# A chunked decay-attention and expert kernel: bonus and state products in quarters of the array, scaling by 1/q0 on ScalarE, another order on TensorE

## The chip, the cores and the metric

One core of a Trainium2 chip runs the kernel. Its engines are called as in the profile: PE is TensorE (PEld its weight loads), DVE is VectorE, ACT is ScalarE, POOL is GpSimd, and SP is the engine that issues most DMAs. The metric is the device time of one execution in microseconds, lower is better. The kernel before has a median of 321.75 us over three runs (320.64 to 328.07).

## What is computed

The first half is a linear attention with a decay that depends on time and channel, for 4 batches, 8 heads, 768 steps and 48 channels. The second sends each of the 3072 rows through at most one of eight small networks.

```python
for t in range(S):
    cur = einsum('bhd,bhe->bhde', u * k[t], v[t])
    y[t] = einsum('bhd,bhde->bhe', r[t], state + cur)
    state = w[t][..., None] * state + einsum('bhd,bhe->bhde', k[t], v[t])
...
logits = x @ w_gate;  e = argmax(logits);  p = softmax(logits)
out = x + (x @ w_skip > 0) * p[e] * (relu(x @ w1[e]) @ w2[e])
```

Everything is kept in fp32 or in pairs of numbers that add up to it.

## The kernel before

**Chunks.** The 768 steps of a batch are cut into 6 chunks of 128, so the attention is 24 chunks, one after the other. Within a chunk the channels of two heads lie on the 128 partitions, one head on 0 to 47 and the other on 64 to 111 (index g), and a counts four such pairs of heads. The state is carried from chunk to chunk; the first chunk of each batch starts without one.

**What one chunk takes.** The helpers have the names that the prediction uses.

- `prep_scan`, `prep_keys`: DVE runs two scans of products of w, `q` from the end (L277) and `rh` from the start (L289), and takes `rq`, 1/q at the chunk's start (L284). POOL makes `kq` = k q (L287).
[...]
- `intra`: PE transposes `kq` (L321), ACT copies the result to `kt` (L323), and PE forms the scores `kq` x `rp` in quarters of the array, 64 rows by 64 columns, into the banks psA0 and psA1 (L328).
- `mask`: DVE multiplies each of the two banks by a triangle, giving `asb` (L334).
- `bonus_sums`, `bonus`: PE multiplies `rk` by u and sums over the channels of each head, with a block-diagonal weight `ubk_sb`, into a bank psB (L343); DVE multiplies by v, held with channels on partitions (`vt`), into the bank psY (L347), which starts y.
- `update`, `carry`: PE adds k v to the state in psu (L356); ACT scales it by the next chunk's q (L366) and copies it to `sblk` (L371), block-diagonal again.
- `outputs`: PE adds `asb` x v (L378) and `sblk` x `rp` (L383) to psY. `evict`: ACT copies psY to `xT` (L388). `rows_out`: PE turns it into rows and router logits (L396). `store`: ACT copies those (L405, L408) and SP writes them out (L410).

**The order.** It is written by hand, in the loop at L595: every engine takes its instructions in the order of the program's text. In step s the loop loads chunk s+4, prepares chunk s+2 (scans and products), forms scores, masks and bonus of chunk s+1, and finishes the outputs of chunk s. On PE a step is update, outputs, transposes, scores, bonus sums, rows_out. On DVE it is the scan q, rq, rh, rp, two masks, bonus. An SP queue holds all chunk loads in program order; a DMA also waits for the one eight places before it, since there are eight semaphores for them.

**Beside the chunks.** After every six chunks a router (L412) finds each row's expert and its place. It is a generator of small steps: `drip` sets some of them between DVE's other work, `pace` says how many, and what they need of PE or ACT is queued in `held` and issued at `flush`. In the first two groups ACT makes the one-hot rows (`mark`, L479), two instructions each, two rows per chunk; later groups make them on DVE (`one_hot`, L474). In some chunks the weights of the first experts are fetched (L90), and ACT and POOL split them into a rounded part and a rest (L107, L273). After the last chunk the experts follow; their products of PE are most of the second half of the span.

## Time and profile before

| what | value |
|---|---|
| median of three runs | 321.75 us |
| the profiled execution | 317.5 us |
| its span, first to last instruction | 315.6 us |
| mean granted clock of PE | 0.986 |
| busy: PE, DVE, ACT, POOL | 292.2, 244.8, 185.3, 115.5 us |
| chain that ended last: PE, DMA, DVE | 72%, 13%, 10% |
| mean DMA rate over the span | 192 GB/s |

In the rows of a timeline stand the start in us from the span's start, the length, the engine, the line, the operation, output<-inputs, sizes as partitions x elements, and a count; in brackets the idle time ahead and what ended it. A row that stands for several instructions gives the time from the first one's start to the last one's end. Grouped rows give the total busy time and the mean length in ns of one, and after the bar the idle time ahead. A product of PE in fp32 shows as two instructions, so four products read x8, and a weight load goes with each. Records of one engine overlap a little, so the distance from start to start is what an instruction costs its engine.

### The profile page before, as it was taken

What the parts mean: (1) busy time and instruction counts of PE and PEld (TensorE: products, weight loads), DVE (VectorE), ACT (ScalarE), POOL (GpSimd) and SP (SyncE); (2) the same over time, 40 slices, a digit from 0 to 9 for tenths busy, and PEclk for the clock granted to TensorE, in tenths of its full rate; (3) what the DMA queues carried; (4) which work ended last, traced back from release to release, by engine and by line L of the source; (5) the groups of instructions that cost most, each with busy time, mean ns of one, the idle gap of its engine ahead of it and who ended that gap; (6) DMA issues with size and microseconds to landing.
All of it is one profiled execution on the core that took longest, in us unless ns stands there. A gap on an engine that the chain in (4) does not pass through costs nothing.

```text
span 315.6 us, 8456 instructions
## 1 busy us (share of the span) xinstructions
PE 292.2 (93%) x3229; PEld 269.6 (85%) x3229; DVE 244.8 (78%) x505; ACT 185.3 (59%) x527; POOL 115.5 (37%) x118
## 2 busy tenths in 40 slices
PE   7499999899898998979999999999999999999992
PEld 2388888788787887868889899999999999999991
DVE  8899999999999999999637479587785949496310
ACT  4437667689775998766633358274564828184200
POOL 8164455555535566543401772411102020101111
PEclk9879999999999999999999999999999999999998
DMA  7999999999899988885301489756657473630001
GB/s 227 220 214 241 232 292 271 257 264 264 212 233 257 267 187 179 180 206 194 116 25 34 143 294 348 275 195 218 213 199 239 152 256 95 243 143 27 6 4 37
DMA packets 23778, 60.45 MB, mean 192 GB/s; under 512 B 4902, under 2 KB 11338, under 8 KB 23728
## 3 DMA queue, kind: packets, MB, share of 16 engines
q1 hardware_dynamic: 21248, 53.69, 62.6%
q0 software_dynamic: 2048, 5.48, 5.3%
q8 instruction: 27, 0.44, 0.7%
q10 hardware_dynamic: 432, 0.66, 0.6%
q14 instruction: 23, 0.19, 0.2%
HBM read 52.76 MB, written 7.86 MB: 192 GB/s over the span
## 4 chain that ended last, share of the span: by engine, by line
PE 72%; DMA 13%; DVE 10%; POOL 1%; issue 1%; ACT 1%; SPq 0%; POOLq 0%; DVEq 0%
DMA wrk<-wrk 10%; PE psO L790 7%; PE psO L788 7%; PE psO L789 7%; PE psY L378 6%; PE psH L770 6%; PE psH L769 6%; PE psH L768 6%; PE psA L328 6%; PE psY L383 5%; PE psB L343 5%; DVE asb L334 4%; PE psH L126 4%; DVE psY L347 3%; PE psT L321 3%; DVE rp L297 2%
## 5 line engine op out<-in xcount | busy, mean ns | idle before, releaser
L775 ACT ACTIVATE hh<-psH 128x256 fp32r<-128x256 f32 x60 | 23.0, 383 | 56.8 <-PE psH L770 53.5
L732 POOL DMA_INDIRECT out<-fin,ids x16 | 17.0, 1065 | 102.5 <-DVE fin L795 94.7
L770 PE MATMUL psH<-xTh,w1l 128*128 128x256 f32 x168 | 47.6, 283 | 0.0
L769 PE MATMUL psH<-xTl,w1h 128*128 128x256 f32 x168 | 47.6, 283 | 0.0
L768 PE MATMUL psH<-xTh,w1h 128*128 128x256 f32 x168 | 47.6, 283 | 0.0
L302 POOL TENSOR_TENSOR rk<-wrk 128x512 f32<-128x512 f32 x24 | 30.6, 1275 | 28.9 <-DVE rp L297 14.5
L788 PE MATMUL psO<-w2h,hh 128*128 128x384 f32 x120 | 40.8, 340 | 0.0
L790 PE MATMUL psO<-w2h,hl 128*128 128x384 f32 x120 | 40.2, 335 | 0.0
L789 PE MATMUL psO<-w2l,hh 128*128 128x384 f32 x120 | 40.2, 335 | 0.0
L378 PE MATMUL psY<-asb,v 128*48 128x128 f32 x384 | 26.6, 282 | 13.1 <-DVE psY L347 13.0
L287 POOL TENSOR_TENSOR kq<-wrk,q 128x512 f32<-128x512 f32 x24 | 28.6, 1190 | 18.5 <-DVE q L277 13.4
L776 DVE SCALAR_TENSOR_TENSOR hl<-psH,hh 128x256 fp32r<-128x256 f32 x60 | 25.2, 420 | 12.5 <-ACT hh L775 12.1
L334 DVE TENSOR_TENSOR asb<-psA,c_sb 128x512 f32<-128x512 f32 x48 | 30.7, 681 | 4.3 <-PE psA L328 4.3
L378 PEld LDWEIGHTS psY<-asb,v 128*48 128x48 f32 x384 | 20.5, 126 | 15.6 <-DVE psY L347 15.4
L297 DVE SCALAR_TENSOR_TENSOR rp<-wrk,rq,rh 128x128 f32<-128x128 f32 x96 | 33.1, 405 | 0.5
L770 PEld LDWEIGHTS psH<-xTh,w1l 128*128 128x128 f32 x168 | 32.2, 192 | 0.0
L769 PEld LDWEIGHTS psH<-xTl,w1h 128*128 128x128 f32 x168 | 32.2, 192 | 0.0
L768 PEld LDWEIGHTS psH<-xTh,w1h 128*128 128x128 f32 x168 | 32.2, 192 | 0.0
L795 DVE SCALAR_TENSOR_TENSOR fin<-psO,gates,xg 128x384 f32<-128x384 f32 x15 | 9.3, 618 | 28.5 <-PE psO L790 28.5
L289 DVE TENSOR_TENSOR_SCAN rh<-wrk,pss 128x516 f32<-128x516 f32 x24 | 28.9, 1205 | 2.6 <-PE pss L516 1.3
L277 DVE TENSOR_TENSOR_SCAN q<-wrk,pss 128x516 f32<-128x516 f32 x24 | 29.1, 1214 | 1.4 <-DMA wrk<-wrk 1.4
L343 PE MATMUL psB<-rk,ubk_sb 128*128 128x128 f32 x192 | 27.8, 288 | 0.9 <-POOL rk L302 0.9
(145 smaller groups left out, 668.6 us busy)
## 6 DMA issues: line engine op xcount, KB each, us to landing
r<-w SPq DMA_DIRECT2D x48, 512.0 KB, 5.8
wrk<-wrk SPq DMA_DIRECT2D x46, 288.9 KB, 6.3
v<-vN SPq DMA_DIRECT2D x24, 192.0 KB, 6.2
out<-x SPq DMA_DIRECT2D x24, 192.0 KB, 5.4
vt<-wrk SPq DMA_DIRECT2D x46, 96.0 KB, 6.1
wrk<-wrk SPq DMA_DIRECT2D x1, 258.5 KB, 3.8
wrk<-wrk ACTq DMA_DIRECT2D x1, 256.0 KB, 4.0
wrk<-wrk SPq DMA_DIRECT2D x1, 256.0 KB, 4.5
```

What stands on the lines that cost most here:

```text
L277: nc.vector.tensor_tensor_scan(q.rearrange("p a j -> p (a j)")[:, ::-1], t[:, 1:1 + NP * CW][:, ::-1], floor, 0.0, op0=ALU.mult, op1=ALU.max)
L297: last = nc.vector.scalar_tensor_tensor(rp[:, a], wk["r"][:, a], wk["rq"][:, a], wk["rh"][:, a, :P], op0=ALU.mult, op1=ALU.mult)
L302: mul = nc.gpsimd.tensor_tensor(rk.rearrange("p a j -> p (a j)"), wk["w"][:, R_OFF:K_OFF], wk["w"][:, K_OFF:V_OFF], op=ALU.mult)
L334: nc.vector.tensor_tensor(s, psa[g], tri.rearrange("p (o j) -> p o j", o=1).to_broadcast([P, NP, P]), op=ALU.mult)
L343: nc.tensor.matmul(wk["psb"][:, a], ubk_sb[:, a], wk["rk"][:, a], start=True, stop=True)
L378: nc.tensor.matmul(psy[64 * g:64 * g + D, a], v[:, 2 * a + g], wk["asb"][g][:, a], start=False, stop=(c == 0), skip_group_check=True)
L768: nc.tensor.matmul(ps, w1h[:, o:o + P], xTh[:, kc], start=(kc == 0), stop=False)
L769: nc.tensor.matmul(ps, w1h[:, o:o + P], xTl[:, kc], start=False, stop=False)
L770: nc.tensor.matmul(ps, w1l[:, o:o + P], xTh[:, kc], start=False, stop=(kc == KC - 1))
L788: nc.tensor.matmul(pso, h[j, fc][0], w2h[:, o], start=(fc == 0), stop=False)
L789: nc.tensor.matmul(pso, h[j, fc][0], w2l[:, o], start=False, stop=False)
L790: nc.tensor.matmul(pso, h[j, fc][1], w2h[:, o], start=False, stop=(fc == FC - 1))
```

## The change

**Quarters.** `ubk_sb` holds u in 64 columns instead of a block-diagonal 128, and the bonus sums become eight products of 64 rows by 64 columns for one chunk instead of four over the whole array (L353). They go into the right halves of psA0 and psA1, from which DVE's masks of the same chunk have been read by then. psB is gone. The state's part of y becomes eight such products too (L400), with `sblk` no longer block-diagonal and copied by one instruction. y lies in two banks, psY0 and psY1, one for each g; the pairs of heads 0, 1 lie on partitions 0 to 47 and 2, 3 on 64 to 111. So bonus (L359) and evict (L407) are two instructions each of 128x256, `vt` is loaded in this layout by four DMAs of 1 KB rows instead of two of 2 KB rows, and the matrix `wgp_sb` by twelve DMAs instead of three.

**1/q0 onto r.** ACT writes r rq into `rp`, four instructions of 128x128 (L296, `scale_reads`), and DVE multiplies by rh in one instruction of 128x512 (L301).

**Order.** Bonus sums and bonus move from the step of the scores to the next step; rows_out moves from the end of a step to the start of the next. The router's one-hot rows are all made on DVE, and its pace for the third group is 3 instead of 2. The small product that POOL makes of the split weights is set beside the bonus of an earlier chunk.

In the rows that follow, tiles carry numbers that tell buffers apart; a scan reads as SCALAR_TENSOR_TENSOR. On DVE, from one chunk's bonus to the next, before:

```order
L347 TENSOR_TENSOR psY<-psB_250,vt_86 128x512
L277 SCALAR_TENSOR_TENSOR q_279<-wrk_85,pss 128x516
L284 RECIPROCAL rq_289<-q_279 128x4
L289 SCALAR_TENSOR_TENSOR rh_293<-wrk_85,pss 128x516
L297 SCALAR_TENSOR_TENSOR rp_295<-wrk_85,rq_289,rh_293 128x128 x4
L334 TENSOR_TENSOR asb_1_327<-psA_110,c_sb 128x512
L334 TENSOR_TENSOR asb_1_329<-psA_111,c_sb 128x512
L347 TENSOR_TENSOR psY<-psB_331,vt_87 128x512
```

and now:

```order
L359 TENSOR_TENSOR psY_109<-psA_111,vt_86 128x256
L359 TENSOR_TENSOR psY_110<-psA_112,vt_86 128x256
L276 SCALAR_TENSOR_TENSOR q_300<-wrk_85,pss 128x516
L283 RECIPROCAL rq_317<-q_300 128x4
L288 SCALAR_TENSOR_TENSOR rh_321<-wrk_85,pss 128x516
L301 TENSOR_TENSOR rp_326<-rp_326,rh_321 128x512
L339 TENSOR_TENSOR asb_1_350<-psA_111,c_sb 128x512
L339 TENSOR_TENSOR asb_1_352<-psA_112,c_sb 128x512
L359 TENSOR_TENSOR psY_109<-psA_111,vt_87 128x256
L359 TENSOR_TENSOR psY_110<-psA_112,vt_87 128x256
```

The bonus that follows the masks belonged to the masks' own chunk in the same step; it still follows them, but in the next step, in two halves, and it reads the banks psA (111 and 112) that the masks have read. The four rp instructions are one.

On ACT, from one chunk's store to its checks, before:

```order
L405 COPY lgs_351<-psX_531 128x18
L408 COPY x_543<-psX_531 128x2x96 x2
L366 ACTIVATE psu<-psu,q_466 128x48 x4
L371 COPY sblk_112<-psu 64x4x48 x2
L388 COPY xT_588<-psY 128x512
L323 COPY kt_595<-psT_590 128x512
L311 ACTIVATE junk_623,viol<-wrk_85,bias_lo 128x512
L313 COPY q0all<-q_561 128x4
```

and now:

```order
L424 COPY lgs_370<-psX_578 128x18
L427 COPY x_584<-psX_578 128x2x2x48 x2
L380 ACTIVATE psu<-psu,q_505 128x48 x4
L383 COPY sblk_113<-psu 128x4x48
L325 COPY kt_618<-psT_613 128x512
L407 COPY xT_642<-psY_109 128x256
L407 COPY xT_642<-psY_110 128x256
L296 ACTIVATE rp_645<-wrk_85,rq_636 128x128 x4
L313 ACTIVATE junk_673,viol<-wrk_85,bias_lo 128x512
L315 COPY q0all<-q_611 128x4
```

The transposed kq (kt) is copied ahead of xT instead of behind it, xT is two rows, and four scalings rp stand between xT and the checks (junk, q0all).

On PE, one chunk from its bonus sums or rows_out to the next scores, before:

```order
L343 MATMUL psB_427<-rk_300,ubk_sb 128x128 x4
L396 MATMUL psX_436<-wgp_sb,xT_398 128x105 x4
L356 MATMUL psu<-v_205,kt_405 48x48 x8
L378 MATMUL psY<-asb_2_423,v_205 48x128
L378 MATMUL psY<-asb_2_425,v_205 48x128 x2
...
L383 MATMUL psY<-rp_295,sblk_112 128x128 x4
L321 MATMUL psT_495<-c_sb,kq_387 128x128 x4
L328 MATMUL psA_110<-rp_391,kq_387 64x128
L328 MATMUL psA_111<-rp_391,kq_387 64x128
```

and now, with L353 and L400 standing for eight rows each:

```order
L415 MATMUL psX_472<-wgp_sb,xT_430 128x105 x4
L370 MATMUL psu<-v_220,kt_406 48x48 x8
L353 MATMUL psA_111<-rk_332,ubk_sb 64x2x64
L353 MATMUL psA_112<-rk_332,ubk_sb 64x2x64
...
L323 MATMUL psT_507<-c_sb,kq_426 128x128 x4
L392 MATMUL psY_109<-asb_2_457,v_220 48x128 x4
L392 MATMUL psY_110<-asb_2_459,v_220 48x128 x4
L400 MATMUL psY_109<-rp_326,sblk_113 48x128
L400 MATMUL psY_110<-rp_326,sblk_113 48x128
...
L333 MATMUL psA_111<-rp_433,kq_426 64x128
L333 MATMUL psA_112<-rp_433,kq_426 64x128
```

The bonus sums stood behind the scores and ahead of rows_out; they now stand behind rows_out and update, and the transposes between them and the outputs.

The core of the difference; the parts left out set up tiles, rename the recording helper `vec` to `nc.vector`, and rename banks.

```diff
@@ loads
                 return
             for g in range(2):
                 nc.sync.dma_start(t[64 * g:64 * g + D], wrk[b, c, g, :, :V_OFF])
-            for g in range(2):
-                nc.sync.dma_start(vf[64 * g:64 * g + D], wrk[b, c, g, :, V_OFF:V_OFF + NP * P])
+
+        def load_vt(i):
+            b, c = seq[i]
+            vt = vt_sb[i % (NBUF + 1)]
+            for c2 in range(2):
+                for g in range(2):
+                    o = V_OFF + 2 * c2 * P
+                    nc.sync.dma_start(vt[64 * c2:64 * c2 + D, 2 * g:2 * g + 2],
+                                      wrk[b, c, g, :, o:o + 2 * P])
...
@@ tiles
-        ubk_sb = keep.tile([P, NP, P], F32, name="ubk_sb")
+        ubk_sb = keep.tile([P, NP, HP], F32, name="ubk_sb")
...
-        psy = ps1.tile([P, NP, P], F32, tag="psY", name="psY")
+
+
+        psy = [ps1.tile([P, 512], F32, tag=f"psY{g}", name=f"psY{g}") for g in range(2)]
+        psy3 = [z[:, :2 * P].rearrange("p (b j) -> p b j", b=2) for z in psy]
         psa = [ps1.tile([P, NP, P], F32, tag=f"psA{g}", name=f"psA{g}") for g in range(2)]
-        sblk = [pers.tile([P, NP, 2, HP], F32, name=f"sblk{i}") for i in range(2)]
+        sblk = [pers.tile([P, NP, HP], F32, name=f"sblk{i}") for i in range(2)]
...
@@ prep
-                if vec.last is not None:
-                    beside(mul, vec.last)
+                beside(nc.gpsimd.tensor_tensor(lo, raw, hi, op=ALU.subtract), work[i - 2]["bonus"])
...
-        def prep_reads(i):
+        def scale_reads(i):
             wk = work[i]
             rp = wk["rp"] = att.tile([P, NP, P], F32, tag="rp", name=f"rp{i}", bufs=3)
             for a in range(NP):
-                last = nc.vector.scalar_tensor_tensor(
-                    rp[:, a], wk["r"][:, a], wk["rq"][:, a], wk["rh"][:, a, :P],
-                    op0=ALU.mult, op1=ALU.mult)
+                nc.scalar.activation(rp[:, a], wk["r"][:, a], AF.Copy, scale=wk["rq"][:, a])
+
+        def prep_reads(i):
+            wk = work[i]
+            rp = wk["rp"]
+            last = nc.vector.tensor_tensor(rp, rp, wk["rh"][:, :, :P], op=ALU.mult)
...
@@ products
+        psb = [z.rearrange("p a (h j) -> p a h j", h=2)[:, :, 1] for z in psa]
+
         def bonus_sums(i):
-            wk = work[i]
-            wk["psb"] = ps1.tile([P, NP, P], F32, tag="psB", name=f"psB{i}")
-            for a in range(NP):
-                nc.tensor.matmul(wk["psb"][:, a], ubk_sb[:, a], wk["rk"][:, a],
-                                 start=True, stop=True)
+            rk = work[i]["rk"].rearrange("p a (h j) -> p a h j", h=2)
+            for a2 in range(2):
+                for c2 in range(2):
+                    for g in range(2):
+                        a, rows = 2 * c2 + a2, slice(64 * g, 64 * g + HP)
+                        nc.tensor.matmul(psb[g][64 * c2:64 * c2 + HP, 2 * a2:2 * a2 + 2],
+                                         ubk_sb[rows, a], rk[rows, a], start=True, stop=True)
 
         def bonus(i):
-            nc.vector.tensor_tensor(psy, work[i]["psb"], vt_sb[i % (NBUF + 1)], op=ALU.mult)
+            vt = vt_sb[i % (NBUF + 1)].rearrange("p a (h j) -> p (a h) j", h=2)
+            for g in range(2):
+                work[i]["bonus"] = nc.vector.tensor_tensor(
+                    psy[g][:, :2 * P].rearrange("p (q j) -> p q j", j=HP), psb[g],
+                    vt[:, 4 * g:4 * g + 4], op=ALU.mult)
...
             nb = sblk[(i + 1) % 2]
-            for g in range(2):
-                rows = slice(64 * g, 64 * g + HP)
-                nc.scalar.copy(nb[rows, :, g, :D], psu[rows, :, :D])
+            nc.scalar.copy(nb[:, :, :D], psu[:, :, :D])
 
         def outputs(i):
             b, c = seq[i]
             wk, v = work[i], v_sb.pop(i)
-            for a in range(NP):
-                for g in ((0, 1), (1, 0))[a % 2]:
-                    nc.tensor.matmul(psy[64 * g:64 * g + D, a], v[:, 2 * a + g],
-                                     wk["asb"][g][:, a], start=False, stop=(c == 0),
-                                     skip_group_check=True)
+            for g in range(2):
+                for a2 in range(2):
+                    for c2 in range(2):
+                        a = 2 * c2 + a2
+                        nc.tensor.matmul(psy3[g][64 * c2:64 * c2 + D, a2], v[:, 2 * a + g],
+                                         wk["asb"][g][:, a], start=False, stop=(c == 0),
+                                         skip_group_check=True)
             if c > 0:
-                for a in range(NP):
-                    nc.tensor.matmul(psy[:, a], sblk[i % 2][:, a], wk["rp"][:, a],
-                                     start=False, stop=True, skip_group_check=True)
+                for a2 in range(2):
+                    for c2 in range(2):
+                        for g in range(2):
+                            a, rows = 2 * c2 + a2, slice(64 * g, 64 * g + HP)
+                            nc.tensor.matmul(psy3[g][64 * c2:64 * c2 + D, a2],
+                                             sblk[i % 2][rows, a, :D], wk["rp"][rows, a],
+                                             start=False, stop=True, skip_group_check=True)
 
         def evict(i):
-            xT = work[i]["xT"] = att.tile([P, NP, P], F32, tag="xT", name=f"xT{i}")
-            nc.scalar.copy(xT, psy)
+            xT = work[i]["xT"] = att.tile([P, 2 * 2, P], F32, tag="xT", name=f"xT{i}")
+            for g in range(2):
+                nc.scalar.copy(xT[:, 2 * g:2 * g + 2], psy3[g])
...
@@ router
-            def mark(c):
-                dd = att.tile([P, 2 * P], BF16, tag="dd", name=f"dd{i0}_{c}")
-                hot = att.tile([P, 2 * P], BF16, tag="hot", name=f"hot{i0}_{c}", bufs=NC)
-                nc.scalar.activation(dd, iota, AF.Square, bias=r1[:, c], scale=-1.0)
-                nc.scalar.activation(hot, dd, AF.Relu, bias=rows1_, scale=-2.0)
-                hots.append(hot)
...
-                if i0 + m >= LATE:
-                    one_hot(c)
-                    yield 1
-                else:
-                    marks.append(lambda c=c: mark(c))
+                one_hot(c)
+                yield 1
...
@@ the loop
                 if s == -1:
                     nc.sync.dma_start(wgs_sb, wgs)
                 if on(s - 1):
+                    rows_out(s - 1)
                     store(s - 1)
+                if on(s):
+                    update(s)
+                    carry(s)
+                    bonus_sums(s)
+                drip(pace[0])
                 for i0, m in GROUPS:
                     if i0 + m == s:
-                        pace[0] = 1 if i0 + m < LATE else 2
+                        pace[0] = 1 if i0 + m < LATE else 3
                         later.append(router(i0, m))
                         if i0 + m == LATE:
                             later.append(early())
                 if on(s):
-                    update(s)
-                    carry(s)
-                drip(pace[0])
+                    bonus(s)
                 if on(s + 2):
                     prep_scan(s + 2)
+                if on(s + 1):
+                    turn(s + 1)
+                flush()
                 if on(s):
                     outputs(s)
-                flush()
                 if on(s + 2):
                     prep_keys(s + 2)
                     drip(2 * pace[0])
-                    prep_reads(s + 2)
                 if on(s):
                     evict(s)
+                if on(s + 2):
+                    scale_reads(s + 2)
+                    prep_reads(s + 2)
                 if on(s + 1):
-                    intra(s + 1)
+                    scores(s + 1)
                     mask(s + 1, 0)
                     mask(s + 1, 1)
-                    bonus_sums(s + 1)
-                    bonus(s + 1)
                     drip(2 * pace[0])
                 if on(s + 2):
                     prep_check(s + 2)
-                for _ in range(min(2, len(marks))):
-                    marks.popleft()()
                 if s == n - 1:
                     early_tokens(0)
-                if on(s):
-                    rows_out(s)
                 flush()
```

110 lines of the change are left out of this document (54 added, 56 removed).

## The prediction

> **What bounds the kernel now.** I read the table of windows first, then the chain that ended last, then the order of time engine by engine. Columns of the first: stretch in us, its length, busy time of PE, PEld, DVE, ACT and POOL with instruction counts, PE's granted clock, DMA share, GB/s.
>
> ```profile
> 24.40:30.20 5.80, 5.80 (x93) 5.18 (x93) 5.45 (x11) 4.08 (x15) 2.44 (x3) 1.00 1.06 237
> ```
>
> This is one lean chunk, without router steps or weight casts. PE is busy throughout, DVE has 0.35 us to spare, ACT 1.7. The chain shows such a chunk's order (start, length, engine, output, line):
>
> ```profile
> 28.86 0.88 PE psY L378 x16
> 29.74 1.09 PE psY L383 x8
> 30.82 0.44 PE psT L321 x4
> 31.26 1.02 PE psA L328 x24
> 32.28 1.09 PE psB L343 x8
> 33.37 0.87 PE psX L396 x8
> 34.24 0.49 PE psu L356 x16
> ```
>
> They add up to 5.88 us: PE and nothing else. In chunks with side work DVE becomes the bound: router steps stand between its own, and where POOL's kq falls on rp, whose four instructions otherwise take 1.14 us, they take
>
> ```profile
> 72.84 2.17 DVE L297 SCALAR_TENSOR_TENSOR rp<-wrk,rq,rh 128x128 f32<-128x128 f32 x4
> ```
>
> The stage that the edit is in runs from chunk 1's first product with v to chunk 23's, 22 chunks:
>
> ```profile
> 22.81 1.05 PE L378 MATMUL psY<-asb,v 128*48 128x128 f32 x16
> ...
> 160.96 1.08 PE L378 MATMUL psY<-asb,v 128*48 128x128 f32 x16
> ```
>
> 138.2 us, or 6.28 a chunk. What follows (the experts) is not edited except for the names of two banks, so I let it move as a block.
>
> **The change part by part.** On PE, L343 and L383 had 4 products each over the whole array; now there are 8 of a quarter each. The nearest row is L328, which is quarters already. Weight loads, lean chunk:
>
> ```profile
> 24.67 0.47 PEld L321 LDWEIGHTS psT<-c_sb,kq 128*128 128x128 f32 x4
> 25.31 0.85 PEld L328 LDWEIGHTS psA<-rp,kq 64*64 64x64 f32 x32 [0.17 <-issue]
> 26.33 0.97 PEld L343 LDWEIGHTS psB<-rk,ubk_sb 128*128 128x128 f32 x8 [0.17 <-issue]
> ...
> 28.65 0.83 PEld L378 LDWEIGHTS psY<-asb,v 128*48 128x48 f32 x16
> 29.66 0.97 PEld L383 LDWEIGHTS psY<-rp,sblk 128*128 128x128 f32 x8 [0.18 <-issue]
> ```
>
> 32 loads of L328 take 0.85 us, so 16 take 0.43, against 1.09 for each of the old groups. That relieves PE by 1.3 us a chunk, and if PE stayed the bound it would count. Bounds of the 0.43: equal to it if four quarters overlap as in L328, 0.85 if only two do.
>
> Each change of array shape leaves 0.17 us without a load (the three "issue" rows). Before, a chunk has four such changes; now rows_out, update, bonus sums, transposes, asb products, state products have six, 0.34 us back. [...]
>
> The other order decides more than these savings. The bonus sums of chunk s now go into the right halves of psA, so they must follow DVE's masks of s, and the bonus products on DVE (L359 of the changed kernel; L296, L301, L353 and L400 below are its lines too) wait for them. Behind it on DVE stand q, rq and rh, then the product rp, which waits for ACT's four scalings; these stand behind ACT's two copies xT, which wait for PE's outputs, which wait for L359. So one loop goes mask, PE, DVE, PE, ACT, DVE, mask, once per chunk. Before, psB had a bank of its own, its sums did not wait for masks, and rp needed nothing of ACT. DVE's rows give pitch (start to start) and length:
>
> ```profile
> 26.47 1.29 DVE L334 TENSOR_TENSOR asb<-psA,c_sb 128x512 f32<-128x512 f32 x2 [0.28 <-PE psA L328]
> 27.67 0.69 DVE L347 TENSOR_TENSOR psY<-psB,vt 128x512 f32<-128x512 f32 x1
> 28.27 1.22 DVE L277 TENSOR_TENSOR_SCAN q<-wrk,pss 128x516 f32<-128x516 f32 x1
> 29.52 0.18 DVE L284 RECIPROCAL rq<-q 128x4 f32<-128x4 f32 x1
> 29.62 1.20 DVE L289 TENSOR_TENSOR_SCAN rh<-wrk,pss 128x516 f32<-128x516 f32 x1
> 30.85 1.14 DVE L297 SCALAR_TENSOR_TENSOR rp<-wrk,rq,rh 128x128 f32<-128x128 f32 x4
> ```
>
> Masks 1.20 pitch, q 1.25, rq 0.10, rh 1.23; a record is 0.09 longer than its pitch. For new shapes, the rows by form:
>
> ```profile
> L560 DVE TENSOR_TENSOR h0l<-hf,h0h 128x512 fp32r<-128x512 f32 x2 | 1.4, 687 | 0.1
> ...
> L776 DVE SCALAR_TENSOR_TENSOR hl<-psH,hh 128x256 fp32r<-128x256 f32 x2 | 0.8, 425 | 1.6 <-ACT hh L775 1.5
> ```
>
> So rp as one 128x512 product costs 0.60 (it replaces 1.14), and each bonus half 0.42, pitch 0.33 (two replace 0.60). DVE saves 0.48 of work. From DVE's end to PE's next load:
>
> ```profile
> 56.81 0.68 DVE L347 TENSOR_TENSOR psY<-psB,vt 128x512 f32<-128x512 f32 x1
> ...
> 57.54 0.83 PEld L378 LDWEIGHTS psY<-asb,v 128*48 128x48 f32 x16 [1.03 <-DVE psY L347]
> ```
>
> 0.05 us. From the last quarter load (25.31 + 0.85) to DVE's mask (26.47): 0.31. ACT:
>
> ```profile
> 24.98 0.59 ACT L388 COPY xT<-psY 128x512 f32<-128x512 f32 x1
> 25.46 0.59 ACT L323 COPY kt<-psT 128x512 f32<-128x512 f32 x1
> ...
> 28.47 0.55 ACT L408 COPY x<-psX 128x192 f32<-128x192 f32 x2
> 28.97 1.20 ACT L366 ACTIVATE psu<-psu,q 128x48 f32<-128x48 f32 x4
> ```
>
> A copy of 512 columns has pitch 0.48, one of 192 has 0.25, so 256 columns about 0.29. No row shows a scaling of 128 columns from SBUF. From above, a 256-column instruction with an operand per partition:
>
> ```profile
> 69.74 0.51 ACT L483 ACTIVATE hot<-dd,c_sb 128x256 bf16<-128x256 bf16 x1
> ...
> 70.15 0.49 ACT L482 ACTIVATE dd<-iota,rall 128x256 bf16<-128x256 bf16 x1
> ```
>
> pitch 0.41, length 0.51. From below, a plain copy brought down to 128 columns: pitch 0.20, length 0.31. The operand adds 0.12 at 256 columns (0.41 against 0.29), so I take pitch 0.30, length 0.40; four take 1.30 us.
>
> The loop, from the first mask's start in us: second mask done 1.29; PE released 1.34; 16 quarter loads 1.77; DVE starts bonus 2.08; first half done 2.50. PE meanwhile: shape change, transposes, shape change, 1.77 + 0.17 + 0.47 + 0.17 = 2.58, so outputs start there; asb 0.83, change 0.18, state 0.43: 4.02; ACT released 4.33; two copies 4.91; four scalings 6.21; DVE starts rp 6.26; next mask **6.86**. DVE alone would have been ready at 2.08 + 0.66 + 1.25 + 0.10 + 1.23 = 5.32; it idles 0.94 there and 0.88 ahead of the bonus. First chunks of a batch have no state product: 0.61 less, 6.25. The last period has no rp: 4.02 + 0.85 + 0.31 = 5.18.
>
> The rest lies beside this loop. ACT gets some 1.3 us of scalings, 0.1 for the second xT, loses one of two sblk copies (0.3, by the 192-column row) and the 24 marking instructions of 0.5 us (L482, L483). ACT's lean chunk goes from 4.1 to 5.2 us, and a cast of 512 columns adds 0.5, inside 6.86; check, cast, store, carry and kt stand between the scalings and the next xT with about 1 us left. If that cover were gone, each 0.1 us would go straight into the loop. The twelve one-hots of the first two groups move from ACT to DVE, each 256 columns, so at most the 0.33 of L776's pitch, and three a chunk. Masks and bonus leave 0.88 idle between them, so at most 0.1 sticks out; these and the router's smaller steps I cost at nothing, at 0.33 each without that cover. PE's router products stand between transposes and outputs, on the loop; bound by
>
> ```profile
> 85.43 0.46 PE L516 MATMUL pss<-sg,hot 128*128 128x40 bf16 x12
> ```
>
> at 0.4, twice in each of three groups: 2.4 us. kq, which starts after q, now ends before rp starts at 6.26, so the clash behind the 2.17 goes. vt is loaded by four DMAs instead of two, wgp by twelve instead of three, all on SP; what stands behind them there (v, out, weights, the next wrk) is issued later. The load that DVE waits for soonest is wrk:
>
> ```profile
> wrk<-wrk SPq DMA_DIRECT2D x46, 288.9 KB, 6.3
> ```
>
> It is issued two chunks (13 us) ahead and lands in 6.3, so I cost the DMAs at nothing; without that cover q waits up to one landing, 6 us once.
>
> Sum: 18 x 6.86 + 3 x 6.25 + 5.18 + 2.4 = 149.8 us against 138.2, **+11.6**. Start (chunk 0's bonus 0.6 later) and end (quicker last state product, -0.3) add 0.3: +12. The profiled execution, 317.5 us, becomes 329.5. The three runs shown have median 321.75, 4.2 above the profiled one, so I forecast **334**.
>
> **The rivals.** (1) DVE's own work closes the loop. Place: the 0.94 us idle before rp; if scalings and copies end by 5.32, the chunk is 5.32 + 0.60 = 5.92 everywhere: 21 x 5.92 + 5.18 = 129.5, -8.4 in all, **313**, faster. For it: PE is relieved of 1.3 us, and the 5.92 needs no new price. Against: the legs on PE and ACT must shrink by 0.94, more than the lower bounds of all of them give. (2) The loop holds with cheap legs: scalings at 0.20 and 0.31 (-0.39), releases of 0.23 instead of 0.31 (-0.16): 6.31, then 18 x 6.31 + 3 x 5.92 + 5.18 + 2.4 = 138.9, **323**, no change. For it: back-to-back ACT rows overlap. Against: the 0.41 row. (3) Quarters run two at a time: +0.43 twice, 7.72 and 6.68 a chunk, +17 more, **351**; L328 speaks against it. (4) In the 12 chunks that fetch weights SP issues 9 DMAs, the weights last; a cast on ACT that waits for them holds up the next xT. At 0.5 us each, +6, **340**. Against: no such wait stands in the rows before.
>
> **How the numbers follow.** Forecast (loop of 6.4 to 7.3 us) 0.58, rival 1 0.12, rival 2 0.17, rival 3 0.05, rival 4 0.08. The forecast's own range, scalings from 0.20 to 0.41, is 326 to 343. Down to 316 it takes in rival 2 and the upper part of 1; up to 345 rival 4. Two per cent, about what a measurement of this kernel can tell from no change, is 6.4 us: slower beyond 328.2 is nearly all of the forecast and rivals 3 and 4, 0.67; within it rival 2, a slice of the forecast and of rival 1, 0.23; faster 0.10.
>
> **What would show it.** Right: lean chunks of 6.9 us; PE no longer busy throughout, near 4.9 us a chunk; on DVE an idle of 0.9 ahead of L359 released by psA's products and of 0.9 ahead of L301 released by L296; xT released by L400; 16 loads of L353 in 0.43. Wrong: L301 waiting for nothing (then rival 1); L296's pitch near 0.2 (rival 2); ACT or DMA named as releaser of the loop's first step; a stage under 138 us.

## The result and the profile after

353.37 us (median of 4 runs, 351.02 to 354.40) against 324.91 (median of 4, 320.64 to 328.38): ratio 1.099, 95% interval 1.089 to 1.109. Slower, as forecast, but outside the range of 316 to 345. One thing is needed to read this: in some executions, of kernels with and without the change, the experts' part takes some 10 us longer (last section), and by their times the changed kernel's four runs and the two of before near 328 are of that kind, while the ratio counts only before's other two, near 321. Runs measured side by side with the same runs of before form a series. In two further series the change costs 22.9 us (e5: 340.41 against 317.49, ratio 1.071, 1.066 to 1.077) and 24.3 us (e13: 352.29 against 327.97, 1.074, 1.070 to 1.077), and there both sides seem alike in this. That is the number to explain: twice the forecast +12.

The first view is the timeline of one lean chunk (start, length, engine, line; idle time ahead and what ended it in brackets; rp is r rq rh, and rk, which POOL makes behind it, is r k):

```profile
40.67 1.28 DVE L339 TENSOR_TENSOR asb<-psA,c_sb 128x512 f32<-128x512 f32 x2
...
42.01 0.42 PEld L353 LDWEIGHTS psA<-rk,ubk_sb 64*64 64x64 f32 x14 [0.35 <-DVE asb L339]
42.60 0.42 PEld L323 LDWEIGHTS psT<-c_sb,kq 128*128 128x128 f32 x4 [0.17 <-issue]
...
42.71 0.76 DVE L359 TENSOR_TENSOR psY<-psA,vt 128x256 f32<-128x256 f32 x2 [0.76 <-PE psA L353]
...
43.20 1.08 PE L392 MATMUL psY<-asb,v 128*48 128x128 f32 x16
...
44.21 0.40 PEld L400 LDWEIGHTS psY<-rp,sblk 64*48 64x48 f32 x16 [0.19 <-issue]
...
44.92 0.65 ACT L407 COPY xT<-psY 128x256 f32<-128x256 f32 x2 [1.01 <-PE psY L400]
45.45 1.28 ACT L296 ACTIVATE rp<-wrk,rq 128x128 f32<-128x128 f32 x4
...
46.76 0.69 DVE L301 TENSOR_TENSOR rp<-rp,rh 128x512 f32<-128x512 f32 x1 [0.83 <-ACT rp L296]
...
47.37 1.28 DVE L339 TENSOR_TENSOR asb<-psA,c_sb 128x512 f32<-128x512 f32 x2
```

This is the loop of the prediction, leg by leg. From the mask's start: bonus at 2.04 (forecast 2.08), outputs 2.53 (2.58), copies 4.25 (4.33), scalings 4.78 (4.91), rp 6.09 (6.26), next mask **6.70** (6.86). Both forecast idle times of DVE are there, 0.76 and 0.83, with the forecast releasers.

The second view is the table of windows (stretch, its length, busy time of PE, PEld, DVE, ACT, POOL with instruction counts, granted clock of PE, DMA share, GB/s): the stage as the prediction bounds it, what follows it, the lean chunk of the first view, and two neighbouring stretches of 3.4 us.

```profile
26.77:182.77 156.00, 126.74 (x2307) 101.24 (x2306) 122.43 (x242) 110.08 (x396) 69.03 (x64) 0.96 0.87 204
182.77:349.20 166.43, 154.30 (x1097) 149.37 (x1097) 96.31 (x199) 73.19 (x167) 32.16 (x31) 0.94 0.44 149
40.67:47.37 6.70, 5.68 (x108) 4.53 (x108) 5.08 (x9) 5.04 (x20) 2.45 (x2) 1.00 0.88 179
30.30:33.70 3.40, 1.03 (x19) 0.63 (x18) 3.14 (x6) 3.08 (x13) 2.15 (x2) 1.00 1.01 157
33.80:37.20 3.40, 3.39 (x30) 2.71 (x32) 2.19 (x5) 1.29 (x4) 0.39 (x2) 0.50 1.10 224
```

The first row's start is chunk 1's first L392, its end chunk 23's. So the difference can be laid beside the forecast's own terms (before: 22.81, 138.15 and 154.64 us):

| stretch | forecast | first profile | e5 | e13 |
|---|---|---|---|---|
| to chunk 1's outputs | +0.6 | +4.0 | +3.0 | +3.6 |
| stage, chunk 1 to 23 | +11.6 | +17.9 | +20.8 | +19.4 |
| from there to the end | -0.3 | +11.8 | +0.1 | +12.0 |

The last row is the longer experts' part, not the change: it is +0.1 in e5. Within the stage the bare loop at measured steps (18 x 6.70, 6.43 + 6.56 + 6.56 where a batch begins, 5.18 at the end) is 145.3 us, +7.2. The last step is 5.18 in the first profile only; in e5 and e13 it is 6.80 and 6.71, at half clock. The other 11 to 14 us stand in a few long chunks. From chunk 18's outputs to chunk 21's, three steps that the bare loop does in 20.1, it takes 26.1, 25.6 and 25.4 us in the three profiles; the rest is chunks 1 to 6 and 10 to 15, not the same ones each time.

Chunk 3's load shows one kind. SP's queue of the same kernel, in which a row is an issue and its length:

```profile
14.17 0.33 SPq L615 DMA_DIRECT2D wgp_sb<-wgp  x1
15.72 1.19 SPq L617 DMA_DIRECT2D wgp_sb<-wgp  x2
...
22.02 1.10 SPq L617 DMA_DIRECT2D wgp_sb<-wgp  x2
23.24 0.97 SPq L157 DMA_DIRECT2D wrk<-wrk  x2
```

That load of wrk in the kernel before, and DVE's q of the changed kernel:

```profile
14.38 0.80 SPq L153 DMA_DIRECT2D wrk<-wrk  x2
```

```profile
29.08 1.23 DVE L276 TENSOR_TENSOR_SCAN q<-wrk,pss 128x516 f32<-128x516 f32 x1 [2.03 <-DMA wrk<-wrk]
```

The twelve wgp loads hold the queue for 9 us, wrk is issued at 23.24 instead of 14.38, and its q waits 2.03 us. In the windows above TensorE is then busy for 1.03 of 3.40 us, and in the next 3.40 its granted clock is 0.50. The other kind, TensorE from chunk 18 on:

```profile
145.80 1.09 PE L333 MATMUL psA<-rp,kq 64*64 64x128 f32 x32
149.21 0.20 PE L461 MATMUL pss<-oh,trib 128*128 128x48 bf16 x1 [2.32 <-DVE oh L458]
...
149.40 1.65 PE L415 MATMUL psX<-wgp_sb,xT 128*128 128x105 f32 x8
150.98 0.88 PE L370 MATMUL psu<-v,kt 128*48 128x48 f32 x16
151.79 1.13 PE L353 MATMUL psA<-rk,ubk_sb 64*64 64x128 f32 x16
...
153.60 1.08 PE L392 MATMUL psY<-asb,v 128*48 128x128 f32 x16
...
162.46 0.18 PE L521 MATMUL pss<-tab,identb 128*128 128x40 bf16 x1 [1.91 <-DVE q L276]
```

and DVE at chunk 18:

```profile
149.07 0.68 DVE L301 TENSOR_TENSOR rp<-rp,rh 128x512 f32<-128x512 f32 x1
149.67 1.28 DVE L339 TENSOR_TENSOR asb<-psA,c_sb 128x512 f32<-128x512 f32 x2
```

The router's rank products (L461) wait 2.32 us for DVE's oh. Behind them in the queue stand row products, state products and the bonus sums, which are on the loop; L415 then takes 1.65 us instead of 1.14, at half clock. The outputs (153.60) come 3.93 us after the mask's start instead of 2.53, 1.4 us late. That chunk is 8.81 us long, against 6.56 for a bare first chunk of a batch; the other 0.8 stand on DVE, where seven router steps, up to oh, lie ahead of rp, which itself waits for nothing. Ahead of chunk 20's outputs, behind its transposes, the router's place products (L521) wait 1.91 us for DVE's q.

### The profile page after: what moved, and what is told of

Read it like the earlier page. It is cut to its first block, busy times and chain, and to the rows that moved or that the text cites. A ratio compares the mean times of both kernels' runs of the same rounds, so it can differ in the third digit from the quotient of the medians.

```text
span 349.2 us, 9280 instructions
## 1 busy us (share of the span) xinstructions
PE 299.7 (86%) x3582; PEld 262.6 (75%) x3582; DVE 235.8 (68%) x469; ACT 195.8 (56%) x602; POOL 113.6 (33%) x117
## 3 DMA queue, kind: packets, MB, share of 16 engines
HBM read 52.76 MB, written 7.86 MB: 174 GB/s over the span
## 4 chain that ended last, share of the span: by engine, by line
PE 53%; DMA 20%; DVE 11%; ACT 5%; SPq 4%; another core or an unknown queue 2%; issue 2%; POOL 1%; ACTq 0%; POOLq 0%; DVEq 0%
DMA wrk<-wrk 13%; PE psH L784 6%; PE psH L783 6%; PE psH L785 6%; PE psO L803 6%; PE psO L805 6%; PE psO L804 6%; DMA vt<-wrk 4%; DVE asb L339 4%; PE psY L392 3%; PE psH L126 3%; PE psA L353 3%; ACT rp L296 2%; DVE q L276 2%
## 5 line engine op out<-in xcount | busy, mean ns | idle before, releaser
L353 PE MATMUL psA<-rk,ubk_sb 64*64 64x128 f32 x384 | 26.8, 306 | 23.6 <-DVE asb L339 21.5
L803 PE MATMUL psO<-w2h,hh 128*128 128x384 f32 x120 | 42.2, 352 | 2.8 <-issue 2.1
L791 DVE SCALAR_TENSOR_TENSOR hl<-psH,hh 128x256 fp32r<-128x256 f32 x60 | 25.2, 420 | 24.9 <-ACT hh L790 18.9
L804 PE MATMUL psO<-w2l,hh 128*128 128x384 f32 x120 | 41.4, 345 | 0.3 <-issue 0.3
L805 PE MATMUL psO<-w2h,hl 128*128 128x384 f32 x120 | 41.2, 343 | 0.3 <-issue 0.2
L353 PEld LDWEIGHTS psA<-rk,ubk_sb 64*64 64x64 f32 x384 | 15.6, 144 | 31.3 <-issue 23.5
L296 ACT ACTIVATE rp<-wrk,rq 128x128 f32<-128x128 f32 x96 | 30.7, 399 | 4.4 <-DVE rq L283 4.3
L783 PEld LDWEIGHTS psH<-xTh,w1h 128*128 128x128 f32 x168 | 33.1, 197 | 0.0
L407 ACT COPY xT<-psY 128x256 f32<-128x256 f32 x48 | 15.8, 376 | 28.1 <-PE psY L400 27.1
L392 PE MATMUL psY<-asb,v 128*48 128x128 f32 x384 | 28.3, 294 | 3.0 <-DVE psY L359 3.0
L301 DVE TENSOR_TENSOR rp<-rp,rh 128x512 f32<-128x512 f32 x24 | 16.6, 691 | 19.3 <-ACT rp L296 19.3
```

Of the source, the lines that this page charges most:

```text
L296: nc.scalar.activation(rp[:, a], wk["r"][:, a], AF.Copy, scale=wk["rq"][:, a])
L353: nc.tensor.matmul(psb[g][64 * c2:64 * c2 + HP, 2 * a2:2 * a2 + 2], ubk_sb[rows, a], rk[rows, a], start=True, stop=True)
L392: nc.tensor.matmul(psy3[g][64 * c2:64 * c2 + D, a2], v[:, 2 * a + g], wk["asb"][g][:, a], start=False, stop=(c == 0), skip_group_check=True)
L783: nc.tensor.matmul(ps, w1h[:, o:o + P], xTh[:, kc], start=(kc == 0), stop=False)
L803: nc.tensor.matmul(pso, h[j, fc][0], w2h[:, o], start=(fc == 0), stop=False)
L804: nc.tensor.matmul(pso, h[j, fc][0], w2l[:, o], start=False, stop=False)
```

## The experiments

My theory from this: the loop is as forecast, and the rest is what queues ahead of it on SP and TensorE, made dearer by TensorE's clock. Rivals were that the start and the router are long for other reasons, and that one part of the change alone makes all of the loss. All ratios are to before in the same series.

**e5 and e13, the changed kernel again** (no edit).

> The changed kernel as it is, on the chip and beside the runs of before that the next three share. In its first profile the experts' part is 156.6 us (145.3, 145.0, 145.5 and 143.8 in the four kernels so far), since three signals of TensorE to ACT's hh come 5.0 us apart at 205.16, 210.15 and 215.15 us, with matmuls that had been recorded from 197.9 to 203.4; half clock follows for 13.7 us. Theory A, this belongs to the program as built and comes each time: 156 us again, clock share about 0.93, 1.09 to 1.11 of before. Rival, it belonged to that execution: 144 to 146 us in the experts' part, clock share about 0.95, 1.06 to 1.08 of before.

> The changed kernel as it is, beside the next three. Theory A: 1.065 to 1.077 of before, as in its second measurement, stage 156 to 159 us with waits for SP's loads, and the experts' part like that of before in the same call. Rival, the first measurement (1.089 to 1.109) is its true size: 1.085 or more.

1.071 and 1.074. In e5 the experts' part was 144.9 us, so the rival of e5 holds (the long one does not come each time); in e13 it was 156.8, and theory A of e13 holds. Before has no trace in that series; its time, 327.97 instead of 317.49, suggests that it had the long part too.

**e1 and e14, fewer DMAs** of the same bytes (the edit in short, not word for word).

```diff
-for q in range(4): dma(wgp_sb[:, q, o:o+2D], ...); for c2 in range(2): dma(wgp_sb[64*c2.., q, r..], ...)
+for a2, o in ((0, 0), (1, E+1)): dma(wgp_sb[:, a2::2, o:o+2D], wgp[:, a2::2, :2D])
+for g, c2: dma(18 neighbouring columns of wgp_sb[64*c2..], wgp[64*g.., 2*c2:2*c2+2, 2D:])
-for c2, g: dma(vt[64*c2.., 2*g:2*g+2], wrk[b, c, g, ...])
+for c2: dma(vt[64*c2..] as (g, a j), wrk[b, c, :, ...] as "d g j")
```

> The changed kernel with the same bytes in fewer DMAs: wgp in six instead of twelve, vt in two a chunk instead of four (chunk 0's two on ACT's queue too). Theory A, the DMAs that were costed at nothing are on the path: in the changed kernel SP issues the twelve from 14.17 to 23.12 us, about 0.6 each, and only then the wrk load that chunk 3's q waits for (issued 23.24, landed 28.96, DVE idle 2.03, TensorE idle 2.3 until 33.30 and then half clock for 3.4 us). Six fewer bring that load 3.5 us forward: no idle ahead of that q, chunk 1 to chunk 2 from 9.14 us to about 7, no half-clock window there, chunk 20's wait for vt (landed 160.54) gone: 353 becomes 343 to 348. Rival, the start is late for another reason (cold TensorE, the loop filling up): 351 to 355 and the same 9 us between chunks 1 and 2. Both leave a steady chunk at 6.70 us.

> The changed kernel with wgp in six DMAs and vt in two, again. Theory A, the DMAs make 4 to 7 us of the loss: 1.2 to 2.2 per cent less than the changed kernel of this call, no chunk between 1 and 10 over 7.0 us but for half clock. Rival, they make none: within 1 per cent of it.

e1: 339.88 us, 1.072 (1.066 to 1.078), no less than the changed kernel in e5, though in its profile chunks 1 to 4 stand 6.7 us apart. Its four times spread from 334.85 to 341.57, so I repeated it beside the changed kernel: 348.80 against 352.29, ratios 1.062 (1.059 to 1.065) and 1.074. The loads make 3.5 us, 1.0%, less than theory A of e14 had. Where these lie stays open: between the profiles of e13 and e14 the start differs by 1.1 us and the stage by only 0.7 (157.5 and 156.9), between those of e5 and e1 the stage by 6.1 (158.9 and 152.9). Chunk 20 still took 9.3 us in e1: its bonus did not wait for vt; TensorE's next router products (L519 of that kernel) stood 1.92 us ahead of its outputs, waiting for DVE.

e1 also shows what half a clock costs by itself. First TensorE's windows in lean chunks, then DVE's rp (L299 of that kernel) in the second of them:

```profile
42.41:45.82 3.41, 1.86 (x34) 1.28 (x31) 2.65 (x6) 2.19 (x11) 1.27 (x1) 1.00 1.07 315
45.82:49.23 3.41, 3.41 (x57) 2.72 (x53) 2.02 (x3) 1.65 (x6) 1.18 (x1) 0.50 1.01 215
```

```profile
49.43 0.69 DVE L299 TENSOR_TENSOR rp<-rp,rh 128x512 f32<-128x512 f32 x1 [1.55 <-ACT rp L294]
```

In the first window TensorE has only the loop's own idle times, 0.91 us ahead of the bonus sums and 0.53 ahead of the outputs, and is busy for 1.86 of 3.41 us; half clock follows, DVE's idle time ahead of rp goes from 0.83 to 1.55, and that chunk takes 7.42 us instead of 6.70. The same place in e14 takes 8.02.

**e2, ACT's scalings ahead of its copies.**

```diff
                     drip(2 * pace[0])
+                    scale_reads(s + 2)
                 if on(s):
                     evict(s)
                 if on(s + 2):
-                    scale_reads(s + 2)
                     prep_reads(s + 2)
```

> The changed kernel with ACT's four scalings issued ahead of its two copies xT instead of behind them. Theory A, the loop runs through ACT in that order: rq is there 4.1 us after the first mask's start, four scalings take 1.28, so rp starts near 5.5 and the next mask near 6.1 instead of 6.70 us; the idle ahead of L301 falls from 0.83 to under 0.3, the stage by 10 to 13 us, the time from 353 to 340-344. Rival, the copies are what TensorE and DVE need sooner, and they are 1.2 us later now: a steady chunk stays at 6.6 us or more and the time at 350 or above.

336.39 us, 1.059 (1.054 to 1.064). DVE in a lean chunk:

```profile
43.52 0.18 DVE L283 RECIPROCAL rq<-q 128x4 f32<-128x4 f32 x1
43.62 1.20 DVE L288 TENSOR_TENSOR_SCAN rh<-wrk,pss 128x516 f32<-128x516 f32 x1
45.05 0.69 DVE L301 TENSOR_TENSOR rp<-rp,rh 128x512 f32<-128x512 f32 x1 [0.23 <-ACT rp L296]
```

The idle ahead of rp falls from 0.83 to 0.23 and lean chunks to 6.15: theory A's mechanism and its chunk. So the loop does run through ACT in that order. The stage is 153.85 all the same, 2 to 5 us less than the changed kernel's and not 10 to 13, since chunks of 7 to 10 us stand between; 23.9 us of it are at half clock.

**e7, rp by DVE alone** (L296 and L301 replaced by the four instructions of before).

> The changed kernel without its part for ACT: rp in four instructions on DVE, as before; quarters, banks and order as changed. Theory A, the two parts of the change are two legs of one loop: without ACT's the loop closes over DVE, 2.08 + 0.66 + 1.25 + 0.10 + 1.23 + 1.14 = 6.46 us a lean chunk instead of 6.70, and more, up to 7.5, where POOL's kq falls on rp or a router step stands between: 0 to 8 us less than the changed kernel beside it, still 1.05 or more of before. Rival, the quarters alone cost nothing and ACT's scalings made all of the loss: 5.9 to 6.1 us a lean chunk and 1.02 or less of before.

335.79 us, 1.061 (1.054 to 1.069); lean chunks of 6.15 to 6.41, others mostly up to 7.1, a few of 7.6 to 10.0. Theory A: what is left of the change (quarters, order, loads, the router's pace) costs most of it, ACT's part in this order 4.6 us more. No run has the quarters with all of the old order, or the new order alone.

**e4, ACT's scalings alone, on the kernel before.**

```diff
-    last = nc.vector.scalar_tensor_tensor(rp[:, a], wk["r"][:, a], wk["rq"][:, a], wk["rh"][:, a, :P], ...)
+    nc.scalar.activation(rp[:, a], wk["r"][:, a], AF.Copy, scale=wk["rq"][:, a])
+last = nc.vector.tensor_tensor(rp, rp, wk["rh"][:, :, :P], op=ALU.mult)
```

> The kernel before with one part of the change alone: 1/q0 put onto r by ACT in four scalings (which stand ahead of its copy xT there), rp one product on DVE. Theory A, that part alone does no harm, since TensorE's 5.88 us bound a lean chunk and DVE is relieved of about 0.5 us a chunk where it was the bound: 310 to 321 us against 322 to 325 of before, DVE idle ahead of rp under 0.5 us. Rival, the scalings make ACT the bound (4.1 us of work and 1.3 more, with casts and marking instructions) or put rp behind ACT: 325 or above.

323.81 us, 1.021 (1.016 to 1.026): slower than before by about 2%, so theory A fell and the rival's mechanism holds (its 325 was counted from before at 322 to 325; in this series before took 317.38). First ACT, then DVE, in a chunk with marks (line numbers of that kernel; L481 and L482 mark, L297 scales, L298 is rp):

```profile
72.33 0.52 ACT L481 ACTIVATE dd<-iota,rall 128x256 bf16<-128x256 bf16 x1
72.88 0.51 ACT L482 ACTIVATE hot<-dd,c_sb 128x256 bf16<-128x256 bf16 x1
73.30 0.49 ACT L481 ACTIVATE dd<-iota,rall 128x256 bf16<-128x256 bf16 x1
73.82 0.51 ACT L482 ACTIVATE hot<-dd,c_sb 128x256 bf16<-128x256 bf16 x1
...
77.23 1.28 ACT L297 ACTIVATE rp<-wrk,rq 128x128 f32<-128x128 f32 x4
```

```profile
78.54 0.69 DVE L298 TENSOR_TENSOR rp<-rp,rh 128x512 f32<-128x512 f32 x1 [3.01 <-ACT rp L297]
```

ACT works without a gap through a chunk of 7.86 us, 1.91 of it marks, and DVE waits 3.01.

**e12 and e16, the same with the one-hot rows of all groups on DVE** (`one_hot(c)` in place of `marks.append(...)`; the changed kernel has that too).

> The kernel before with ACT's scalings and, as in the changed kernel, the one-hot rows of the first two groups on DVE instead of two marking instructions each on ACT. Theory A, the scalings cost time in the run with them alone because ACT was full there: a chunk with marks and a cast took 7.86 us, ACT without a gap, 1.91 of it marks, DVE idle 3.0 ahead of rp. Without marks such a chunk is ACT's 5.95, DVE's 5.6 or TensorE's 5.88 us: the four chunks at 7.9 come down to 6.0-6.4, 312 to 319 us, 0.985 to 1.005 of before. Rival, ACT's scalings hold rp in every chunk with side work, marks or not: 320 or above, 1.01 or more.

> The kernel before with ACT's scalings and with the one-hot rows on DVE, again. Theory A, its stage is 135.0 us against 138.2 and the rest is the same: 0.985 to 0.995 of before. Rival, that gain was chance of the other call: 0.996 or more.

e12: 324.99 us where before took 326.79 to 328.96 in ten of eleven runs and 320.12 in the other; both forecasts in us were made for short experts' parts, and this one was 154.3. e16: 325.14 against 327.97, **0.991** (0.988 to 0.993), a gain of under 1% whose interval excludes 1. DVE in e12, where e4 has the 3.01:

```profile
75.23 0.26 DVE L205 TENSOR_SCALAR hot<-iota,rall 128x256 bf16<-128x256 bf16 x1
75.78 0.69 DVE L298 TENSOR_TENSOR rp<-rp,rh 128x512 f32<-128x512 f32 x1 [0.29 <-ACT rp L297]
```

The chunks at 7.9 us are 6.0 to 6.1 now and the stage 135.0 against 138.2. These two parts of the change pay together, if they come without the rest; no run has the one-hot rows on DVE alone.

**e6, three edits**: e1's loads, e2's order and two router steps at a place instead of three (`pace[0]` 3 to 2).

> The changed kernel with three edits together: fewer DMAs (six for wgp, two for vt), ACT's scalings ahead of its copies, and two router steps instead of three at each of the places in a chunk for the group that ends at chunk 18 (as before). Theory A, what is left over the loop in the two runs with one edit each is waits on SP's queue and on this router: chunks at 6.15 us nearly throughout, chunks 18 to 21 in 20 us instead of 25.4, stage 1 to 23 about 136 to 140 us, experts 145, together 317 to 324 us (1.00 to 1.02 of before). Rival, TensorE's idle time ahead of the masks and its half-clock windows stay whatever the queue does: stage 146 or more, 328 or above.

325.89 us, 1.028 (1.024 to 1.032); stage 142.1, between the two forecasts: chunks of 6.15 to 6.6 up to chunk 18, where theory A failed. TensorE there, and the windows around it:

```profile
131.66 1.09 PE L331 MATMUL psA<-rp,kq 64*64 64x128 f32 x32
136.74 0.20 PE L459 MATMUL pss<-oh,trib 128*128 128x48 bf16 x1 [3.99 <-DVE oh L456]
...
136.93 1.78 PE L413 MATMUL psX<-wgp_sb,xT 128*128 128x105 f32 x8
```

```profile
133.80:137.20 3.40, 0.46 (x9) 0.46 (x10) 3.07 (x11) 1.25 (x6) 1.27 (x1) 1.00 0.67 155
137.20:140.60 3.40, 3.40 (x41) 2.79 (x41) 0.00 (x0) 1.48 (x7) 0.00 (x0) 0.50 0.88 183
```

With fewer router steps at a place oh comes later, and the products already in TensorE's queue wait 3.99 us, then run at half clock; DVE does nothing in the second window, as it waits for TensorE.

**e10 and e15, the router's products behind the transposes**, not at the chunk's end: e10 on e6 with three steps again, e15 on the changed kernel.

```diff
-                flush()
+                flush(s >= n - 1)      # at the chunk's end: all but ranks and places
```

> The six-fold kernel with the router's products (ranks and places) issued only behind the transposes in the middle of a chunk, no longer at its end ahead of the next row products, and three router steps at each place as in the changed kernel. Theory A, in the six-fold run TensorE stands 3.99 us at the first rank product until DVE's oh is there (136.74), with the row products, state products and bonus sums of the chunk behind it, and half clock follows: 10.48 us for that chunk instead of 6.15. Behind the transposes oh is there first: chunks 18 to 21 in 19 to 20.5 us instead of 23.8, stage 137 to 139.5 instead of 142.1, 1.008 to 1.018 of before instead of 1.028. Rival, DVE's router steps themselves make these chunks long: 23 us or more for the three and 1.024 or above.

> The changed kernel with the router's products issued behind the transposes in the middle of a chunk, and nothing else. Theory A, their place ahead of the row products makes the long chunks 18 to 21: 25.4 us come down to 21 to 22 and the time by 3 to 5 us (1.0 to 1.6 per cent). Rival, as in the six-fold kernel with this edit, what those three chunks gain the other groups' chunks and the end lose: within 1 per cent of the changed kernel.

e10: 336.13 us, in the series where before took 327.58 (median) and experts' parts were long (155.3 us; 145.4 in e6). Chunks 18 to 21 took 18.9 us instead of 23.8, less than theory A had, and the stage had no half clock left. But it is 141.3 against e6's 142.1, since chunks 7, 11, 13 and 17 took 7.9 to 8.1, each followed by one of 4.9 to 5.3. e15 is **slower**: 358.15, 1.091 (1.088 to 1.094), 1.7% above e13. There too chunks 18 to 21 came down, to 22.1 us from 25.4, as theory A had it, but the stage is 163.8 against 157.5: chunks 7 and 13 took 8.4 and chunk 11 took 9.7. TensorE in e15 at chunk 7:

```profile
76.93 0.66 PE L325 MATMUL psT<-c_sb,kq 128*128 128x128 f32 x4
78.98 0.18 PE L463 MATMUL pss<-oh,trib 128*128 128x48 bf16 x1 [1.40 <-DVE q L278]
...
79.23 1.74 PE L394 MATMUL psY<-asb,v 128*48 128x128 f32 x16
```

The rank products now stand directly ahead of the outputs and wait there, for DVE's instructions up to q by the semaphore, although oh was done at 74.06 (q reads pss, the tile that they write). Both places lie on the loop; moving the wait along it won 3 to 5 us at chunks 18 to 21 and lost most of that, or more, at others.

**e9 and e11, three products with zeros on TensorE while it waits for the masks**, on the changed kernel and on e10.

> The changed kernel with three products with zeros (bf16, 512 columns, 0.22 us each, into the bank that the transposes are about to overwrite) on TensorE ahead of the bonus sums, where it waits for the masks. Theory A, the clock: in the nine profiles so far TensorE's half-clock windows last 3.4 us or multiples of it, and 39 of 39 follow a stretch of 3.4 us in which TensorE was busy for under 62%, against 7 stretches under 60% that none followed; the changed loop keeps it near 75%, so each wait drops it. With 0.65 us more in each 6.7 us few stretches fall under 62%: the granted share goes from 0.945-0.953 to 0.965 or more, and 1.071 of before to 1.045-1.060, with the loop still at 6.70. Rival, the windows follow from long waits (a late load, the router's products, 2 to 4 us) that 0.65 us do not bridge: share and time as they were, 1.065 to 1.085.

> The router kernel of this call with the three products with zeros ahead of the bonus sums too. Theory A (the clock) has TensorE above 62% everywhere and the share at 0.98 or more, but at 6.15 us a chunk TensorE waits for masks less than 0.65 us: the fillers lengthen the chunk by 0 to 0.3 us, so the sum is within 3 us of the run without them. Rival, they lie wholly in waiting time and what half clock is left goes: 3 to 5 us less than without.

e9: 351.89 us with a clock share of 0.943, 0.4 us from the changed kernel in e13 (352.29, 0.934; another series), and 13.7 us at half clock within the stage in the one and about 17 in the other: the rival's numbers. Its reason, long waits, holds only in part. Half clock in e9 begins at 47.15, 91.53 and 163.21 us; in the 3.41 us ahead of the first two TensorE was busy for 1.70 and 1.86 us, and no idle time there is longer than 1.2 us. So 0.65 us of fillers (0.217 us each, the distance from one such product of L598 to the next at 6.54 us of the first profile) did not keep the clock up in e9, and half clock came behind the loop's ordinary waits there too, as in e1. e11 is a miss for both: 344.51 against e10's 336.13, stage 151.1; lean chunks grew from 6.15 to up to 6.8 us, and e10's stage had no half clock to win back.

**e3 and e8, the bonus sums in the free columns of the y banks**, with the old order (sums behind the scores, product behind the masks); e8 on e6.

```diff
-psb = [z.rearrange("p a (h j) -> p a h j", h=2)[:, :, 1] for z in psa]
+psb = [z[:, 2 * P:].rearrange("p (a j) -> p a j", j=HP) for z in psy]
```

> The changed kernel with the bonus sums in the unused columns 256 to 511 of the two y banks, so that they need not wait for DVE's masks, and in the old place of the order (sums behind the scores, product behind the masks). Theory A, the wait on the masks is the loop's other leg: the 0.76 us idle ahead of L359 goes, outputs start 2.0 us after the mask's start instead of 2.53, and a steady chunk falls from 6.70 to about 6.3 us: 353 becomes 343 to 347. Rival, only the leg over ACT counts and the freed time turns up as a longer idle ahead of L301: 6.6 us or more a chunk, 350 or above.

> The six-fold kernel with the bonus sums in columns 256 to 511 of the y banks and in the old place of the order; a product with zeros over columns 0 to 255 opens each bank's chunk, so that the sums behind it need no start of their own and the bonus stays in y (in the run with its own columns alone it was left out of y). Theory A, without the wait on the masks the chunk is 5.85 to 6.0 us, TensorE being the next bound: stage 128 to 134, 308 to 317 us, 0.97 to 1.00 of before. Rival, the sums now wait for ACT's copies xT (the same banks), which stand behind the scalings: 6.15 us or more a chunk, no better than the six-fold kernel.

In e3 the bonus is missing from y. 331.71 us, 1.045 (1.040 to 1.050): several chunks near 5.85 us, below theory A's 6.3. e8: 325.96, 1.026 (1.019 to 1.033), no better than e6 (1.028), though several chunks take 5.6 to 5.9. Its TensorE:

```profile
41.21 0.54 PE L348 MATMUL psY<-warm 128*128 128x256 bf16 x2 [0.58 <-ACT xT L409]
41.69 0.67 PE L354 MATMUL psY<-rk,ubk_sb 64*64 64x128 f32 x16
42.28 1.14 PE L417 MATMUL psX<-wgp_sb,xT 128*128 128x105 f32 x8
```

The rival's wait: the products that open the banks stand until ACT has copied xT out of them. That need not be all: e8's stage has 17.1 us of half clock, e6's 3.4.

## Why the prediction was wrong

The mechanism was right. The loop and its releasers came as worked out, at 6.70 us (6.86) a chunk and 145.3 (147.4) in all; 16 quarter loads of L400 take 0.40 (0.43); four scalings 1.28 (1.30); a shape change on the loop costs 0.17 to 0.19, as in the rows of before; the last step is 5.18 (5.18) where the clock is full. One sign did not come: TensorE is busy for 5.68 of a lean chunk's 6.70 us, not near 4.9. Rival 1 fell with the 0.83 us of idle ahead of rp, rival 2 with 6.70 against its 6.31, rival 3 with the 0.40. Rival 4 is there but small: one cast waited 2.5 us for weights in the first profile.

The step that failed is "The rest lies beside this loop", which makes the sum of 149.8 fall 6 to 9 us short of the stage: it put 2.4 us beside the loop, and 11 to 14 came. Three terms were wrong or missing.

- The router's products, "at 0.4, twice in each of three groups: 2.4 us". That counted their work. They also wait in TensorE's queue, the rank products behind the scores for DVE's oh (2.32 us, 3.99 in e6), the place products ahead of the outputs for DVE's q (1.91), with the loop's products behind them: 5.3 to 6.0 us beyond the bare loop at chunks 18 to 21 alone. At chunk 18 that wait makes 1.4 us, and DVE's router steps ahead of rp, costed at nothing, 0.8. With the products moved (e15) those three chunks take 3.2 us less, but others more, so no run is without the wait.
- The DMAs, at nothing. I did write down the uncovered case, "6 us once". The cover of 13 us was itself queued behind twelve issues; in e14 half as many wgp and vt loads save 3.5 us over the whole run.
- The clock had no term. Before, TensorE was busy for 129 of 138 us and the stage ran at full clock; after, 127 of 156, at 0.96. One window at half clock cost 0.7 us in e1 and 1.3 in e14; with the four or five of them in the changed kernel's stage that is an estimated 3 to 7 us.

How the 11 to 14 us divide between these is not settled: the three chunks bound the router's third group, the loads' share of the stage is anything from 0.7 to 6, and half clock lies partly within both. The start, +0.6 forecast, came out at +3.0 to +4.0: chunk 0's rp waits 2.0 us for ACT in the first profile, and the next q starts 1.9 us later than before (12.38 against 10.45), waiting for its load.

A second slip is in the last step. I added 4.2 us because the median of the three runs shown, 321.75, stood above the profiled execution. No run shows what those 4.2 us are: in two later series before took 316.6 to 318.7 but for one run. And the 10 us between the two kinds of execution, which 328.07 among the three runs hinted at, had no place in the sum.

## What to carry to other kernels

When an engine stops being the bound and becomes one leg of a loop over several engines, its spare time is no sure cover: an instruction in its queue that waits for another engine delays the loop by what of its wait exceeds the slack there, however little its work (2.32 us of wait made 1.4 at chunk 18, half clock included), and TensorE can lose its full clock as well (0.46 us of work in 3.40 us of e6, then a granted 0.50). So list for each queue on the loop, SP's too, what stands ahead of the loop's next step and what that waits for. And try the parts of a change apart: scalings on ACT cost 2.1% alone, came out 0.9% ahead together with one-hot rows on DVE, and cost 4.6 us in the order in which they came.
